# Retention and SwiGLU feed-forward in one kernel: weight chunks issued by SP, and four attention jobs and one norm moved to other places

## The chip, the cores and the metric

The kernel runs on one core of a Trainium2 chip. Its time is device microseconds of one launch, compiled kernel alone. Several executions are timed in rounds that alternate with the kernel before on the same chip; the median is quoted, with the lowest and highest run. One execution of each kernel is also recorded by the hardware profiler; moments below ("at 240.5 us") are from the start of that execution. The engines are TensorE (PE in the profile), the vector engine DVE, the scalar engine ACT, GpSimd (POOL) and SP, which here only issues transfers. A bank is the place where TensorE leaves a product until DVE or ACT has taken it out (its eviction).

## The reference

```python
# q, k, v: 8 batches x 8 heads x 576 positions x 64
scores = (q @ k.T) / sqrt(64)
Dmat = where(i >= j, gamma[h] ** (i - j), 0)       # gamma[h] = 1 - 2 ** (-5 - h)
attn = (scores * Dmat) @ v                          # retention, no softmax
x = attn.transpose(0, 2, 1, 3).reshape(4608, 512)
xn = x / sqrt(mean(x * x, -1) + 1e-6) * rms_g
g, val = xn @ w_gate, xn @ w_val                    # 512 -> 1536
out = (g * sigmoid(g) * val) @ w_out                # 1536 -> 512
```

The weights come as float64 and are turned into float32 on the chip.

## The kernel before

The attention is done in jobs (two heads of a stretch of positions), the feed-forward in units of 384 rows. Units 0 and 1 run first with plain products, while the weights still arrive; from unit 2 (the third) on the products are of the Strassen kind, seven block products in place of eight. The change touches the stretch up to the third unit's start, at about 258 us of 1147.

**Weights** come in 18 chunks of 1 MB. Each is loaded into one of four rooms, split by DVE (exponent, mantissa, sign) and ACT, and joined. A new chunk is issued once an earlier one has left its room:

```python
def load_chunks(n, queue=nc.scalar):                 # before: issued by ACT
    nonlocal n_loads
    while n_loads < min(n, len(chunks)) and waits_at.get(spare(n_loads)) is None:
        load_chunk(n_loads, queue)
        n_loads += 1

def rounding():
    for i in range(len(chunks)):
        ...                                          # exponent(i), (i + 1)
        yield from mantissa(i)                       # DVE; ends with waits_at[room] = None
        load_chunks(i + 5 if i else 0)
        ...
        join(i)
```

**Jobs.** `slot(j)` gives TensorE the values of job j-1 and the scores of job j, and DVE the weighing. `following(j)` is two things: `prepare(j+1)` (two transposes on DVE, the scaling of v on ACT) and the 13 loads of job j+2 on SP. Jobs 0 to 7 are done first. The later ones are put among the 48 steps of the up products of units 0 and 1, and among the first outs:

```python
LATER_AT = (29, 33, 37, 41, 45)

def later(step):
    if step == LATER_AT[0] - 8:
        following(2 * NHP - 1)                       # NHP = 4
    elif step in LATER_AT:
        j = 2 * NHP + LATER_AT.index(step)
        if j < LATER_JOBS:                           # LATER_JOBS = 12
            slot(j, rest=(j > 2 * NHP))
            if j + 1 < LATER_JOBS:
                following(j)
        else:
            values(j - 1)
            carried(j - 1)
```

**First outs.** `across(u)` is the last product of unit u, in seven blocks of 24 matmuls (3.9 us each). Every finished quarter is added up and transposed by DVE and stored with 8 DMAs on SP, 32 for a unit. The third unit's norm stands in `across(1)`. While GpSimd's `combine` makes the Strassen blocks of the up weights, with 12 additions for each of the two matrices:

```python
rest = across(1)
next(rest)
following(LATER_JOBS - 1)
for i, _ in enumerate(rest):
    if i == 1:
        norm_0(2)                    # ACT: four squares; DVE adds them up
        differences(0)
    elif i == 2:
        norm_1(2)                    # TensorE: mean; DVE, GpSimd: root
        diagonals(2)
    elif i == 4:
        norm_2(2)                    # DVE: four scalings, four subtractions
rest = across(0)
next(rest)
combine(1)
slot(LATER_JOBS, rest=False)
following(LATER_JOBS)
for _ in rest:
    pass
combine(0)
slot(LATER_JOBS + 1)
...                                  # third unit follows

def combine(m):
    for g in range(NG):              # NG = 3
        ...
            nc.gpsimd.tensor_tensor(out=o, in0=a, in1=b, op=op)
```

From the fourth unit on the norm's root is computed in another way (`root_1`, `root_2`): a product with ones, a guess at the root by ACT, and polishing on DVE and ACT.

Of the kernel before, what the change touches and what calls it, by code (L numbers as in the profile page):

```python
# [13 lines left out]
ALU = mybir.AluOpType  # L14
# [27 lines left out]
def kernel(  # L42
# [11 lines left out]
    nc = tc.nc  # L54
# [3 lines left out]
    NHP = H // 2  # L58
# [12 lines left out]
    K0, K1 = 2.38924456, 0.703952253  # L71
# [40 lines left out]
    rms_g = const.tile([P, NHP], F32, name="rms_g")  # L112
    rms_k = const.tile([P, NHP], F32, name="rms_k")
# [22 lines left out]
    LATER_JOBS = 3 * NHP  # L136
# [245 lines left out]
    def values(j):  # L382

        d = st[j]
        _, _, c0, c1 = jobs[j]
        av = d["av"] = [bank(f"av_{j}_{i}") for i in range(2)]
        for c in range(c0, c1):
            i, odd = divmod(c, 2)
            for e in range(2):
                mm = nc.tensor.matmul(  # L390
                    av[odd][column(j, odd, e), i * L : i * L + L],
                    lhsT=d["v"][side(odd), i, e] if c < NC - 1 else d["vt"][:, e],
                    rhs=d["ret"][side(odd), e, i],
                    start=(c < c0 + 2), stop=False, skip_group_check=True,
                )


        if j == LATER_JOBS:
            d["valued"] = nc.scalar.copy(out=tick, in_=mhalf[:1])
        else:  # L400
            d["valued"] = nc.gpsimd.memset(tick, 0.0)
        follow(d["valued"], mm)
# [39 lines left out]
    def slot(j, rest=True):  # L442

        if j > len(jobs):
            return
        if rest and j > 0:
            values(j - 1)
        if j < len(jobs):
            scores(j)
            states(j)  # L450
        if j < len(jobs):
            weigh(j)
        if j < 2 * NHP:
            sums(j)
        if rest and j > 0:
            carried(j - 1)
        if 2 * NHP <= j < len(jobs):
            sums(j)
# [10 lines left out]
    def following(j):  # L469
        prepare_next(j)  # L470
        load_next(j)
# [7 lines left out]

    def gather(u, c, sq):  # L480

        if c == NHP - 1 and u > 2:
            nc.vector.scalar_tensor_tensor(
                out=t_of[u], in0=t_of[u], scalar=EPS * DM / P, in1=sq, op0=ALU.add, op1=ALU.add
            )
        elif c:
            nc.vector.tensor_tensor(out=t_of[u], in0=t_of[u], in1=sq, op=ALU.add)
        else:
            t_of[u] = sq

    def norm_0(u):
        for c in range(NHP):
            gather(u, c, square(u, c))

    def norm_1(u):

        ms = bank(f"ms_{u}")
        for s in range(NS):
            nc.tensor.matmul(
                ms[:, s : s + 1], lhsT=t_of[u][:, s * P : s * P + P], rhs=mean_w,  # L500
                start=True, stop=True,
            )
        r = tmp.tile([P, NS], F32, tag="r", name=f"r_{u}", bufs=1)
        nc.vector.tensor_scalar(out=r, in0=ms[:, :NS], scalar1=EPS, scalar2=None, op0=ALU.add)
        nc.gpsimd.tensor_tensor(out=r, in0=r, in1=mhalf.to_broadcast([P, NS]), op=ALU.pow)
        t_of[u] = r
# [36 lines left out]
    def diagonals(u):  # L543
        r = t_of[u]
        t_of[u] = temp(f"diag_{u}")
        for s in range(NS):
            nc.vector.tensor_scalar(
                out=t_of[u][:, s * P : s * P + P], in0=ident, scalar1=r[:, s : s + 1],
                scalar2=None, op0=ALU.mult,
            )  # L550

    def norm_2(u):



        x = x_of[u]
        g = rms_k
        rb = t_of[u]
        if u < 3:
            g = rms_g  # L560
            rb = bank(f"rb_{u}")[:, :U]
            nc.tensor.matmul(rb, lhsT=ones, rhs=t_of[u], start=True, stop=True)
        for c in range(NHP):
            nc.vector.scalar_tensor_tensor(
                out=x[:, c], in0=x[:, c], scalar=g[:, c : c + 1], in1=rb,
                op0=ALU.mult, op1=ALU.mult,
            )
        if u < 2:
            return
        b11, b12 = x[:, :2, :HU], x[:, :2, HU:]  # L570
        b21, b22 = x[:, 2:, :HU], x[:, 2:, HU:]
        t = ffn.tile([P, 3, 2, HU], F32, tag="sums", name=f"sums_{u}")
        t2, t3, t4 = (t[:, i] for i in range(3))
        for o, a, b in ((t3, b22, b12), (b12, b12, b11), (t2, b22, b12), (t4, b21, t2)):
            nc.vector.tensor_tensor(out=o, in0=a, in1=b, op=ALU.subtract)

        t_of[u] = b11, b21, b12, t4, t2, t3, b22
# [97 lines left out]
    def keep(blk, t):  # L675
        nc.sync.dma_start(out=w_blocks[blk], in_=t)
# [27 lines left out]
    def differences(u):  # L704

        h = h_of[u]
        b11, b12, b22 = h[:, :NH, :HU], h[:, :NH, HU:], h[:, NH:, HU:]
        t1 = t1_of[u] = ffn.tile([P, NH, HU], F32, tag="t1", name=f"t1_{u}")
        for o, a, b in ((t1, b12, b11), (b12, b22, b12)):
            nc.vector.tensor_tensor(out=o, in0=a, in1=b, op=ALU.subtract)  # L710
# [146 lines left out]
    def load_chunks(n, queue=nc.scalar):  # L857
# [5 lines that stand above are left out]
# [69 lines left out]
    def rounding():  # L932

        nonlocal n_chunks
        for i in range(len(chunks)):
            if i not in exp_of and i in words_of:
                exponent(i)
                yield
            for ahead in (True, False):
                if i + 1 in words_of and i + 1 not in exp_of and i > (1 if ahead else 0):  # L940
                    exponent(i + 1)
                    yield
                if ahead:
                    yield from mantissa(i)
                    load_chunks(i + 5 if i else 0)
                    yield
            join(i)
            n_chunks += 1
            yield

    steps = rounding()
    LATER_AT = (29, 33, 37, 41, 45)

    def weights(n):

# [10 lines left out]
    def start():  # L966
# [33 lines left out]
        def later(step):  # L1000

            if step == LATER_AT[0] - 8:
                following(2 * NHP - 1)
            elif step in LATER_AT:
                j = 2 * NHP + LATER_AT.index(step)
                if j < LATER_JOBS:
                    slot(j, rest=(j > 2 * NHP))
                    if j + 1 < LATER_JOBS:
                        following(j)
                else:  # L1010
                    values(j - 1)
                    carried(j - 1)

        for j in range(2 * NHP):
            slot(j)
# [50 lines left out]
            pass  # L1066
        for blk, t in first_blocks.items():
            keep(blk, t)
        rest = across(1)
        next(rest)  # L1070
        following(LATER_JOBS - 1)
        for i, _ in enumerate(rest):
            if i == 1:
                norm_0(2)
                differences(0)
            elif i == 2:
                norm_1(2)
                diagonals(2)
            elif i == 4:
                norm_2(2)  # L1080
        rest = across(0)
        next(rest)
        combine(1)
        slot(LATER_JOBS, rest=False)
        following(LATER_JOBS)
        for _ in rest:
            pass
        combine(0)
        slot(LATER_JOBS + 1)
        load_next(LATER_JOBS + 1)  # L1090
# [18 lines left out]

    with tc.manual_schedule():  # L1110
        start()
        nc.vector.tensor_scalar(
            out=rms_k, in0=rms_g, scalar1=3.0 / 8.0 * K1, scalar2=None, op0=ALU.mult
        )
        for u in range(2, NU):
            for i in range(2 * NG):
                for n, _ in enumerate(up(u, i % 2, i // 2)):
                    if n == 2 and turns:
                        prepare_next(turns.pop())
                if i in (1, 3):  # L1120
                    fetch()
                    fetch()
                if i == 2 * NG - 1:
                    rest = across(u)
                    next(rest)
                behind(u, i)
            for i, _ in enumerate(rest):
                if i == 0 and turns:
                    prepare_next(turns.pop())
                if i == 2:  # L1130
                    behind(u, 6)
                    at, n = SLOTS[u % 3]
                    if 2 * NG - 1 in at:
                        load_next(NHP + u // 3 * 8 + n + len(at) - 1)
                elif i == 3 and u + 1 < NU:
                    root_2(u + 1)
                elif i == 4:
                    behind(u, 7)
# [27 lines left out]
```

## Time and profile before

| | before |
|---|---|
| median time, us | 1148.0 (1146.6 to 1148.8, 4 runs) |
| span of the profiled execution, us | 1147.0 |
| TensorE busy | 98 % |
| first outs start (`xo<-w_val`, L726) | 198.75 us |
| third unit's first product (L595) | 258.41 us |

TensorE is the bound: from 258 us on it hardly stands still. Two more are needed later. They are from the timelines of DVE and GpSimd (POOL) of the kernel before; the columns are start, duration, engine, line, operation, what is written and read, shapes, count, and in brackets the wait before it:

```profile
224.85 0.56 DVE L575 TENSOR_TENSOR sums<-x,sums 128x384 f32<-128x384 f32 x1
```

### The profile page before, as it was taken

How to read it: one execution, taken by the hardware profiler on the slowest of the kernel's cores; microseconds unless marked ns; L12 is line 12 of the kernel's file. 1: busy time of each engine (PE TensorE's matmuls, PEld its weight loads, DVE VectorE, ACT ScalarE, POOL GpSimd, SP SyncE). 2: the span in 40 equal slices, each digit the busy share in tenths (PEclk: the TensorE clock that was granted, in tenths of full speed). 3: DMA queues.
4: the chain of work that ended last, by engine and by line, in shares of the span. 5: the costliest groups of instructions: out<-in, count | busy, mean ns of one | idle time of the engine just before them, and what ended most of it. 6: DMA issues, size and time to landing. Idle time of an engine off the chain costs nothing.

```text
span 1147.0 us, 24779 instructions
## 1 busy us (share of the span) xinstructions
PE 1121.7 (98%) x10454; PEld 1045.3 (91%) x10454; DVE 733.4 (64%) x1452; ACT 257.8 (22%) x508; POOL 40.1 (4%) x68
## 2 busy tenths in 40 slices
PE   7899988999999999999999999999999999999998
PEld 6655645999999999999999999999999999999998
DVE  5888777747586586466766776466577576446353
ACT  5456531102211221121221121120221211120210
POOL 0100000190000000000000000000000000000000
PEclk9899998999999999999999999999999999999999
DMA  9844555434553555035345456305336413303304
GB/s 218 214 143 136 143 133 152 121 69 108 136 120 61 163 130 139 35 95 112 97 100 93 111 127 139 119 16 130 101 98 140 122 42 94 128 1 97 125 1 111
DMA packets 307039, 126.72 MB, mean 110 GB/s; under 512 B 284528, under 2 KB 289904, under 8 KB 306928
## 3 DMA queue, kind: packets, MB, share of 16 engines
q1 hardware_dynamic: 296784, 108.98, 38.9%
q10 hardware_dynamic: 10144, 16.16, 4.4%
q8 instruction: 82, 1.34, 0.5%
q14 instruction: 29, 0.24, 0.1%
HBM read 110.14 MB, written 14.94 MB: 109 GB/s over the span
## 4 chain that ended last, share of the span: by engine, by line
PE 93%; DVE 3%; DMA 2%; ACT 1%; issue 1%; SPq 0%; POOL 0%; DVEq 0%; POOLq 0%; ACTq 0%
PE x L595 14%; PE w L595 14%; PE z L595 14%; PE up L652 9%; PE xo L726 8%; PE wo L726 8%; PE zo L726 8%; PE y L595 7%; PE yo L726 4%; PE av L390 2%; PE av L412 2%; PE s L307 1%; PE s L329 1%; DMA w_gate<-in_moe_w_out_dram 1%; DMA w_out<-in_moe_w_out_dram 1%
## 5 line engine op out<-in xcount | busy, mean ns | idle before, releaser
L619 ACT COPY m<-x 128x384 f32<-128x384 f32 x60 | 28.8, 479 | 337.9 <-PE x L595 337.9
L726 PE MATMUL xo<-h,w_out 128*128 128x192 f32 x528 | 90.3, 328 | 0.0
L595 PE MATMUL w<-sums,w_val 128*128 128x192 f32 x480 | 88.7, 328 | 0.3
L595 PE MATMUL x<-x,w_val 128*128 128x192 f32 x480 | 88.8, 328 | 0.0
L595 PE MATMUL x<-x,w_gate 128*128 128x192 f32 x480 | 88.5, 328 | 0.0
L595 PE MATMUL w<-sums,w_gate 128*128 128x192 f32 x480 | 87.9, 326 | 0.0
L595 PE MATMUL z<-x,w_val 128*128 128x192 f32 x480 | 87.8, 326 | 0.0
L595 PE MATMUL z<-x,w_gate 128*128 128x192 f32 x480 | 87.8, 326 | 0.0
L726 PEld LDWEIGHTS xo<-h,w_out 128*128 128x128 f32 x528 | 85.9, 190 | 0.6
L726 PE MATMUL wo<-h,w_out 128*128 128x192 f32 x504 | 85.6, 326 | 0.4 <-DVE c_last L774 0.4
L602 DVE TENSOR_TENSOR u<-m,y 128x384 f32<-128x384 f32 x60 | 33.1, 552 | 78.6 <-PE y L595 78.6
L726 PEld LDWEIGHTS wo<-h,w_out 128*128 128x128 f32 x504 | 82.5, 190 | 0.7 <-DVE c_last L774 0.7
L595 PEld LDWEIGHTS w<-sums,w_val 128*128 128x128 f32 x480 | 79.2, 190 | 2.7 <-DVE c L602 2.7
L595 PEld LDWEIGHTS x<-x,w_val 128*128 128x128 f32 x480 | 79.2, 190 | 0.6
L595 PEld LDWEIGHTS x<-x,w_gate 128*128 128x128 f32 x480 | 79.3, 190 | 0.5
L595 PEld LDWEIGHTS z<-x,w_val 128*128 128x128 f32 x480 | 79.7, 190 | 0.0
L595 PEld LDWEIGHTS z<-x,w_gate 128*128 128x128 f32 x480 | 79.7, 190 | 0.0
L595 PEld LDWEIGHTS w<-sums,w_gate 128*128 128x128 f32 x480 | 79.5, 190 | 0.1
L602 DVE TENSOR_TENSOR h<-u,w 128x384 f32<-128x384 f32 x60 | 33.0, 550 | 69.4 <-PE w L595 69.4
L652 PE MATMUL up<-x,w_gate 128*128 128x384 f32 x192 | 65.8, 499 | 4.9 <-DVE x L435 3.6
L614 ACT ACTIVATE h<-h 128x384 f32<-128x384 f32 x90 | 47.0, 523 | 88.6 <-DVE h L602 88.6
L652 PE MATMUL up<-x,w_val 128*128 128x384 f32 x192 | 65.6, 501 | 1.3 <-DVE h L658 1.3
(189 smaller groups left out, 1783.1 us busy)
## 6 DMA issues: line engine op xcount, KB each, us to landing
w_out<-w_blocks SPq DMA_DIRECT2D x70, 768.0 KB, 4.9
out_dram<-o SPq DMA_DIRECT2D x364, 24.0 KB, 1.6
qraw<-in_q_dram SPq DMA_DIRECT2D x96, 72.0 KB, 2.6
kraw<-in_k_dram SPq DMA_DIRECT2D x96, 72.0 KB, 2.9
k<-in_k_dram SPq DMA_DIRECT2D x48, 128.0 KB, 2.9
v<-in_v_dram SPq DMA_DIRECT2D x48, 128.0 KB, 3.0
w_out<-in_moe_w_gate_dram ACTq DMA_DIRECT2D x5, 1024.0 KB, 5.8
w_out<-in_moe_w_out_dram ACTq DMA_DIRECT2D x3, 1024.0 KB, 6.0
```

What stands on the lines that cost most here:

```text
L307: nc.tensor.matmul(s[side(odd), e, i * L : i * L + L], lhsT=d["kT"][side(e), c * L : c * L + L], rhs=d["qT"][side(e), c * L : c * L + L], ...
L329: nc.tensor.matmul(o[side(e)], lhsT=d["k"][side(odd), i, e], rhs=d["v"][side(odd), i, e], start=True, stop=True,)
L390: mm = nc.tensor.matmul(av[odd][column(j, odd, e), i * L : i * L + L], lhsT=d["v"][side(odd), i, e] if c < NC - 1 else d["vt"][:, e], rhs= ...
L412: mm = nc.tensor.matmul(av[odd][column(j, odd, e), i * L : i * L + L], lhsT=d["sum"][c - 1][side(e)], rhs=d["qT"][side(e), c * L : c * L + L],
L595: nc.tensor.matmul(ps[:, i * HU : i * HU + HU], lhsT=w_up[m][:, 2 * blk + c, cut], rhs=t_of[u][blk][:, c], start=(start and i == c == 0), ...
L602: nc.vector.tensor_tensor(out=o, in0=a, in1=pairs_of(ps), op=ALU.add)
L614: nc.scalar.activation(out=o, in_=c, func=AF.Silu)
L619: nc.scalar.copy(out=s1, in_=pairs_of(x_))
L652: nc.tensor.matmul(ps[:, :U], lhsT=w_up[m][:, 4 * half + c, i * P : i * P + P], rhs=x_of[u][:, c], start=(c == 0), stop=(c == NHP - 1),)
L726: nc.tensor.matmul(ps[:, i * HU : i * HU + HU], lhsT=a[:, c, i * P : i * P + P], rhs=rhs[:, c], start=(start and i == c == 0), stop=False, ...
```

## The change

The intent: SP issues the chunks, so ACT need not stand still for them. Only two of the later jobs (8 and 9) stay among the up products, where the chunk chain leaves DVE no room. Two more (10 and 11) go among the first outs, where TensorE is full and DVE has time. The third unit's norm goes behind them, in the form that all later units use.

```diff
@@ values @@
-        if j == LATER_JOBS:
+        if LATER_JOBS - 2 < j <= LATER_JOBS:
             d["valued"] = nc.scalar.copy(out=tick, in_=mhalf[:1])
         else:
             d["valued"] = nc.gpsimd.memset(tick, 0.0)
@@ gather @@
-        if c == NHP - 1 and u > 2:
+        if c == NHP - 1 and u > 1:
@@ norm_2 @@
-        if u < 3:
+        if u < 2:
@@ rounding @@
-                    load_chunks(i + 5 if i else 0)
+                    load_chunks(i + 5 if i else 0, nc.sync)
@@
-    LATER_AT = (29, 33, 37, 41, 45)
+    LATER_AT = (33, 41)
@@ later @@
-                if j < LATER_JOBS:
-                    slot(j, rest=(j > 2 * NHP))
-                    if j + 1 < LATER_JOBS:
-                        following(j)
-                else:
-                    values(j - 1)
-                    carried(j - 1)
+                slot(j, rest=(j > 2 * NHP))
+                following(j)
@@ start @@
+        nc.vector.tensor_scalar(
+            out=rms_k, in0=rms_g, scalar1=3.0 / 8.0 * K1, scalar2=None, op0=ALU.mult
+        )
         rest = across(1)
         next(rest)
+        for i, _ in enumerate(rest):
+            if i == 0:
+                slot(LATER_JOBS - 2)
+                following(LATER_JOBS - 2)
+            elif i == 1:
+                differences(0)
+        slot(LATER_JOBS - 1)
         following(LATER_JOBS - 1)
-        for i, _ in enumerate(rest):
-            if i == 1:
-                norm_0(2)
-                differences(0)
-            elif i == 2:
-                norm_1(2)
-                diagonals(2)
-            elif i == 4:
-                norm_2(2)
         rest = across(0)
         next(rest)
         combine(1)
-        slot(LATER_JOBS, rest=False)
-        following(LATER_JOBS)
-        for _ in rest:
-            pass
+        for i, _ in enumerate(rest):
+            if i == 0:
+                slot(LATER_JOBS)
+                following(LATER_JOBS)
+            elif i == 1:
+                norm_0(2)
+            elif i == 2:
+                root_1(2)
+            elif i == 3:
+                root_2(2)
+            elif i == 4:
+                norm_2(2)
         combine(0)
```

(`rms_k` was set behind `start()` before; that line moved up. Line numbers are those of each kernel's own text.)

More of the change, by code (lines that the diff above doesn't have):

```diff
@@ L1111 @@
         start()
-        nc.vector.tensor_scalar(
-            out=rms_k, in0=rms_g, scalar1=3.0 / 8.0 * K1, scalar2=None, op0=ALU.mult
-        )
         for u in range(2, NU):
```

## The prediction

> **What bounds the kernel now.** I read the page's slices first, then the windows of the first 400 us, then what TensorE waited for, then the timelines of TensorE, ACT, DVE and the DMA queue between 100 and 262 us. The page:
>
> ```profile
> PE 1121.7 (98%) x10454; PEld 1045.3 (91%) x10454; DVE 733.4 (64%) x1452; ACT 257.8 (22%) x508; POOL 40.1 (4%) x68
> PE   7899988999999999999999999999999999999998
> PEclk9899998999999999999999999999999999999999
> ```
>
> From slice 8 on (230 us) TensorE is full and its clock is whole; the change touches nothing there. What can be won or lost lies before 260 us. In that stage the waits of TensorE from 135 us on, longest first, and two windows (columns: PE, PEld, DVE, ACT, POOL busy, PEclk, DMA share, GB/s):
>
> ```profile
> PE up L652 <- DVE x L435: 3.6, 1, 3.6
> PE av L390 <- ACT w_val L660: 3.5, 1, 3.5
> PE up L652 <- DVE h L658: 1.3, 1, 1.3
> 150.00:154.00 4.00, 4.00 (x8) 2.12 (x8) 3.86 (x9) 3.50 (x8) 0.00 (x0) 0.59 0.62 231
> 176.00:184.00 8.00, 6.71 (x80) 4.38 (x75) 6.74 (x15) 2.70 (x7) 0.09 (x1) 0.50 0.57 189
> ```
>
> So 3.6+3.5+1.3 = 8.4 us idle, and after both long gaps the clock is at half. The timelines show why the gaps are there (start, duration, then the wait before it):
>
> ```profile
> 165.78 0.37 ACTq L855 DMA_DIRECT2D w_gate<-in_moe_w_out_dram  x1
> 172.72 0.69 DVE L871 TENSOR_SCALAR w_gate<-w_gate 128x1024 uint32<-128x1024 uint32 x1 [6.98 <-DMA w_gate<-in_moe_w_out_dram]
> 173.45 1.15 ACT L887 ACTIVATE w_gate<-w_gate,least 128x1024 f32<-128x1024 uint32 x1 [10.58 <-DVE w_gate L871]
> 174.50 0.47 ACT L660 ACTIVATE w_val<-up 128x384 f32<-128x384 f32 x1
> 175.03 0.71 PE L390 MATMUL av<-ret,v 64*64 64x64 f32 x16 [3.52 <-ACT w_val L660]
> 179.20 12.95 PE L652 MATMUL up<-x,w_val 128*128 128x384 f32 x32 [1.28 <-DVE h L658]
> 198.75 4.06 PE L726 MATMUL xo<-w_val,w_out 128*128 128x192 f32 x24
> ```
>
> The last of 18 weight chunks is loaded only when an earlier one has left its staging room (165.78), lands 7 us later, is split by DVE and ACT, and the SiLU behind it in ACT's order frees a PSUM bank late. A chain of chunks, not TensorE, sets the pace from 137 to 179 us.
>
> **The Trainium skill.** "TensorE: Matmul & The Clock Gate", Part 1, says that an idle window of about 3.4 us halves the clock; the trace agrees (gaps of 3.6 and 3.5 us, then 0.59 and 0.50). The same page, under "Architectural detail", calls ACT and DVE strict FIFO; the trace agrees: the SiLU at 174.50 ran behind the 10.58 us wait. "DMA: Bandwidth & Descriptors", "Issuing engines are not separate DMA queues", says that another issuing engine saves only sequencer time; here an issue took 0.37 us on ACT, and what counts is rather what it waits for and stands behind. Nothing in the profile before tests that for SP.
>
> **Part 1: chunks issued by SP.** ACT loses ten issues of about 0.4 us, and no longer stands still until DVE frees the staging room. That alone frees no bank at 172 us: ACT would then wait at the exponent's activation for the same landing. On SP a chunk stands behind the 13 loads of q, k and v of a job. Such a set took 108.62 to 117.13, 151.61 to 159.19 and 204.55 to 212.60: 8 us. From the order of emission, chunk 14 comes right behind the set for job 9, which moves from step 21 to step 25. (Step n: four products into one bank, 2.66 us; step 29 ends at 129.75.) DVE's two transposes for job 8 then end at 121, the first frees the room at 120.6, the set runs to 128.5 and chunk 14 lands at about 134 (5 us after its issue; chunk 14 took 4.8 before). DVE gets to it at 130 and stalls 4 us. TensorE doesn't: five banks give it steps 30 to 34.
>
> **Part 2: jobs 8 and 9 at steps 33 and 41, none at 29, 37 and 45.** Before, job 8 at step 29 cost DVE 3.3 us (0.76+0.27+0.91+0.28 for weights and sums, 1.1 for transposes), and jobs 9 and 10 some 4.5 us each, all inside the chunk chain. Walking the chain on with durations of the trace (0.6 + 0.6 + 1.23 + 1.22 + 1.2 for a chunk's five DVE steps, 5.1 from issue to landing): chunk 15 issued 138.9, lands 144; chunk 16 issued 147.9, lands 152.9; job 8 on DVE to 151.2; chunk 16 freed at 161; SP has by then issued job 10's set (150.7 to 158.7), so chunk 17 goes at 161.1 and lands 166.2, against 165.78 and 172.7 before, when it shared the DMA engines with job 12's set. Its SiLU ends at 168.5. TensorE has run steps 30 to 41 with job 8's 1.0 us between and 0.8 us of waiting for a bank, to 163.5. So the two gaps become one of about 4.5 us. Then as before: 2.9 us for the rest of the job at half clock, a wait for the product with h (DVE, 173.1), 12.95 for steps 42 to 45, and 5.3 for the last two steps, without the 1.4 us of job 11's values: the first outs start at **191.4 instead of 198.75**, a gain of 7.3 us.
>
> **Part 3: two jobs among the first outs.** From there TensorE is full, so what is put there costs. Across(1): seven products of 3.9 = 27.3, plus job 10 at 1.7 (141.24 to 142.93 before). Then job 11 1.7, a product 3.9, job 12 with job 11's values about 1.9, two products 7.8. The sum, 27.3+1.7+1.7+3.9+1.9+7.8, is 44.3: TensorE stands before the new norm's product at 191.4+44.3 = 235.7. Before, the same stretches held 1.4 us for the norm's two small products and 1.2 for job 12's scores, 2.6 in all, against 5.3+0.65 now.
>
> **Part 4: the norm behind them.** Here I expect the gain to go. Job 13's loads stand on SP behind the 32 stores of the first outs, and the norm's squares stand on ACT behind the scaling of job 13's v. Lines of before that size this:
>
> ```profile
> 204.55 2.94 SPq L156 DMA_DIRECT2D qraw<-in_q_dram  x4
> 210.85 0.99 SPq L224 DMA_DIRECT2D v<-in_v_dram  x2
> 213.80 0.51 ACT L285 ACTIVATE v<-v,gv 128x256 f32<-128x256 f32 x1 [8.81 <-DMA v<-in_v_dram]
> 217.59 16.95 SPq L763 DMA_DIRECT2D out_dram<-o  x32
> 203.22 1.76 ACT L477 ACTIVATE sq<-x 128x384 f32<-128x384 f32 x4
> ```
>
> The first out result is there 2.4 us after the fourth product (as 217.56 against 215.18 before): 191.4+17.3+2.4 = 211.1. Thirty-two stores take 16.95: SP is free at 228. The set of job 13 issues v 6.3 us later (210.85-204.55), v lands 2.9 after that (213.80-210.85): 237.2. Scaling ends at 239.1, four squares 1.8, the last addition 0.6: **241.5**. TensorE idles 241.5-235.7 = **5.8 us**, is throttled for some 4 us after it (2 us lost), then the product 0.65, four products 15.6, job 13 2.25 (256.16 to 258.41): the third unit starts at 262.0 instead of 258.41. DVE is done with the norm by then: it has 15.6 us for some 12 us of additions, roots and scaling. So **+3.6 us**: 1147.4+3.6 = 1151.0 us. In one sum: -7.3 (part 2) +3.4 (part 3: 5.95-2.6) +7.8 (part 4) = +3.9, the same within my rounding.
>
> **Rivals.** (a) The norm is not held up, because job 13's loads get out between stores or the squares are ready in time: -7.3+3.4 = -3.9, about 1143.5. For it: ACT ran its scaling early elsewhere (177.32 for a transpose at 203.75). Against it: SP's stores ran with no gap for 16.95 us, and loads are emitted behind them. (b) SP's line makes the chunk chain later, not earlier: if a load set takes the 9 to 11 us that the one from 133.56 to 145.10 took, chunk 14 and all after it come 3 us later and chunk 17 is held too; the gain of part 2 halves: about 1155. For it: a set waits on landings. Against it: fewer transfers overlap now. (c) The chain gets shorter than I think since ACT is never blocked: the gap at 163.5 vanishes (4.5 us and 2 of clock), and with my part 4 the sum is 1144.5. Against it: DVE still waits for chunk 15 and 17 to land, whoever issues them.
>
> **Range and chances.** The terms are each sure to 2 or 3 us, and two of them cancel. Rivals (a), (b) and (c) end at 1143.5, 1155 and 1144.5, so 8 in 10 lie in 1142 to 1156. Two per cent is 23 us; the whole idle and throttled time before 260 us that is in play is some 14 us on either side, so chances: faster 0.01, same 0.98, slower 0.01.
>
> **What would show each step.** Part 1: chunk 14 issued by SP right behind 13 loads, near 128.5, and DVE waiting some 4 us for its landing. Part 2: no gap near 146; one gap of 4 to 5 us near 164 released by ACT's SiLU; first out at about 191. Part 4: a gap of about 6 us before the product with ones over sq, released by ACT or DVE, ACT waiting for v before the squares, and PEclk at 0.5 behind it; the third unit's first product at about 262. I am wrong if that gap is under 2 us, if the first outs start after 195, or if anything past 262 us differs by over 1 us.

## More of the kernel before

```profile
225.98 16.86 POOL L930 TENSOR_TENSOR w_val<-w_val 128x512 f32<-128x512 f32 x12 [13.68 <-PE wo L726]
```

The last subtraction of the third unit's norm ends at 225.4 us. The first twelve additions of `combine` begin at 225.98 us. Before the change, the norm was over when GpSimd began.

## The result, and the profile after

The changed kernel took 1156.3 us (1155.1 to 1157.8, 4 runs) against 1148.0. The ratio is 1.0074, 95 % interval 1.0057 to 1.0092: slower by 0.7 %, "the same" by the 2 % rule, and 0.3 us above the range.

| | before | predicted | after |
|---|---|---|---|
| median time, us | 1148.0 | 1151.0 | 1156.3 |
| profiled span, us | 1147.0 | | 1154.2 |
| first outs start, us | 198.75 | 191.4 | 187.64 |
| TensorE stands before the norm's product, us | | 5.8 | 7.76 |
| third unit's first product, us | 258.41 | 262.0 | 262.78 |
| ACT's copy for the third unit's fourth group, us | 289.80 | +3.6 | 296.46 (+6.66) |

The page of the changed kernel, busy times and the clock's row of its slices:

```profile
PE 1121.1 (97%) x10448; PEld 1045.9 (91%) x10448; DVE 738.6 (64%) x1453; ACT 259.4 (22%) x512; POOL 40.1 (3%) x66
...
PEclk9899999989999999999999999999999999999999
```

Beside the second slice, which is low in both, the slice with a lower clock moved from the seventh (172 to 201 us) to the ninth (231 to 260 us): one trouble went, another came. TensorE's busy time, in which slow products count in full, is equal (1121.1 against 1121.7), so the loss shows as waits. Its waits from 160 to 300 us in the changed kernel (what it waited for: total, times, longest):

```profile
PE ms L513 <- DVE sq L483: 7.8, 1, 7.8
PE av L390 <- ACT w_val L660: 4.4, 1, 4.4
PE up L652 <- DVE h L658: 1.3, 1, 1.3
PE z L595 <- DVE x L435: 1.0, 1, 1.0
PE x L595 <- DVE c L736: 0.6, 1, 0.6
```

Of the two gaps of 3.6 and 3.5 us before the first outs one is left, of 4.4. The 7.8 us ahead of the norm's product are new, and so are the last two lines, which stand at the third unit's start. TensorE's timeline of the changed kernel:

```profile
167.88 0.71 PE L390 MATMUL av<-ret,v 64*64 64x64 f32 x16 [4.45 <-ACT w_val L660]
...
172.05 15.75 PE L652 MATMUL up<-x,w_val 128*128 128x384 f32 x48 [1.28 <-DVE h L658]
187.64 4.06 PE L726 MATMUL xo<-w_val,w_out 128*128 128x192 f32 x24
...
240.50 1.62 PE L513 MATMUL ms<-sq,ones 128*128 128x384 f32 x2 [7.76 <-DVE sq L483]
241.91 6.14 PE L726 MATMUL yo<-h,w_gate 128*128 128x192 f32 x24
...
262.78 1.57 PE L595 MATMUL x<-x,w_gate 128*128 128x192 f32 x8 [0.59 <-DVE c L736]
```

And why the squares came late: SP's queue, then ACT, both of the changed kernel.

```profile
128.60 0.54 SPq L855 DMA_DIRECT2D w_gate<-in_moe_w_out_dram  x1
...
160.70 0.38 SPq L855 DMA_DIRECT2D w_gate<-in_moe_w_out_dram  x1
...
207.76 18.29 SPq L763 DMA_DIRECT2D out_dram<-o  x32
...
232.82 0.99 SPq L224 DMA_DIRECT2D v<-in_v_dram  x2
```

```profile
235.56 0.51 ACT L285 ACTIVATE v<-v,gv 128x256 f32<-128x256 f32 x1 [11.93 <-DMA v<-in_v_dram]
...
237.25 1.74 ACT L477 ACTIVATE sq<-x 128x384 f32<-128x384 f32 x4
```

The 32 stores hold SP from 207.76 to 226.05; only then can the next job's loads go. Its v is issued at 232.82 and ACT, which has waited 11.93 us for it, scales it from 235.56 on. The squares stand behind the scaling in ACT's order, though their input was written by 226.4. Then the clock, in windows of four microseconds (length, then PE, PEld, DVE, ACT, POOL busy, granted clock, DMA share, GB/s):

```profile
240.00:244.00 4.00, 3.50 (x9) 2.93 (x10) 0.99 (x3) 1.10 (x2) 0.00 (x0) 0.50 0.69 150
244.00:248.00 4.00, 4.00 (x20) 4.00 (x19) 0.47 (x1) 0.52 (x1) 0.47 (x1) 0.74 0.00 0
```

Half clock in the first window and for 2.1 of the second window's 4 us ((1 - 0.74) / 0.5 x 4): the block product `yo` takes 5.97 us from start to start (241.91 to 247.88) instead of 3.9.

Last, DVE and GpSimd at the end of the norm in the changed kernel:

```profile
251.83 1.52 DVE L538 SCALAR_TENSOR_TENSOR ms<-e,sq 128x384 f32<-128x384 f32 x1
...
258.61 1.51 DVE L575 TENSOR_TENSOR x<-x 128x384 f32<-128x384 f32 x1
...
261.70 0.56 DVE L575 TENSOR_TENSOR sums<-x,sums 128x384 f32<-128x384 f32 x1
```

```profile
234.66 3.95 POOL L930 TENSOR_TENSOR w_gate<-w_gate 128x512 f32<-128x512 f32 x3
247.53 13.72 POOL L930 TENSOR_TENSOR w_gate<-w_gate 128x512 f32<-128x512 f32 x9 [8.93 <-issue]
```

The same subtraction takes 1.51 us while GpSimd adds beside it and 0.56 once GpSimd is done (261.25). GpSimd stood from 238.6 to 247.53. The profile names no releaser; the blocks that it writes are read by `across(0)`'s first four products, and it went on 0.5 us before the last of them (`yo`) ended at 248.05, so this is probably what held it.

### The profile page after: what moved, and what is told of

Read it like the earlier page. It is cut to its first block, busy times and chain, and to the rows that moved or that the text cites. A ratio compares the mean times of both kernels' runs of the same rounds, so it can differ in the third digit from the quotient of the medians.

```text
span 1154.2 us, 24764 instructions
## 1 busy us (share of the span) xinstructions
PE 1121.1 (97%) x10448; PEld 1045.9 (91%) x10448; DVE 738.6 (64%) x1453; ACT 259.4 (22%) x512; POOL 40.1 (3%) x66
## 4 chain that ended last, share of the span: by engine, by line
PE 88%; DVE 6%; DMA 3%; ACT 1%; issue 1%; SPq 1%; POOL 0%; DVEq 0%; POOLq 0%; ACTq 0%
PE w L595 13%; PE x L595 13%; PE z L595 13%; PE xo L726 8%; PE zo L726 8%; PE wo L726 8%; PE up L652 7%; PE y L595 7%; PE yo L726 4%; PE av L390 2%; PE av L412 1%; PE s L307 1%; DMA w_gate<-in_moe_w_out_dram 1%; PE s L329 1%; DVE w_gate L908 1%
## 5 line engine op out<-in xcount | busy, mean ns | idle before, releaser
L652 PE MATMUL up<-x,w_val 128*128 128x384 f32 x192 | 62.7, 487 | 1.3 <-DVE h L658 1.3
```

The costliest lines, as they stand in the source:

```text
L652: nc.tensor.matmul(ps[:, :U], lhsT=w_up[m][:, 4 * half + c, i * P : i * P + P], rhs=x_of[u][:, c], start=(c == 0), stop=(c == NHP - 1),)
```

## The experiments

Twelve kernels ran, five rounds each, all correct, in four groups that each had their own runs of the kernel before. "After" is the changed kernel.

| kernel | median (lowest to highest), us | ratio to before, 95 % |
|---|---|---|
| after | 1156.3 (1155.1 to 1157.8) | 1.0074 (1.0057 to 1.0092) |
| squares_first | 1149.45 (1149.0 to 1150.9) | 1.0025 (1.0008 to 1.0042) |
| sp_only | 1155.18 (1154.2 to 1156.6) | 1.0072 (1.0056 to 1.0087) |
| act_issue | 1152.99 (1150.6 to 1154.7) | 1.0049 (1.0032 to 1.0065) |
| set_early | 1153.06 (1150.2 to 1153.5) | 1.0046 (1.0030 to 1.0063) |
| root_first | 1148.94 (1146.6 to 1150.1) | 1.0012 (0.9995 to 1.0029) |
| act_root_first | 1143.60 (1142.1 to 1147.0) | 0.9976 (0.9959 to 0.9992) |
| stores_split | 1161.77 (1160.3 to 1161.9) | 1.0124 (1.0104 to 1.0144) |
| act_root2_first | 1145.10 (1144.8 to 1145.6) | 0.9983 (0.9969 to 0.9998) |
| old_norm | 1145.29 (1144.0 to 1146.7) | 0.9978 (0.9963 to 0.9993) |
| after_combine_behind | 1155.57 (1153.5 to 1156.8) | 1.0070 (1.0055 to 1.0086) |
| combine_behind | 1141.05 (1139.9 to 1142.1) | 0.9943 (0.9928 to 0.9959) |
| act_root_again | 1144.91 (1143.8 to 1146.2) | 0.9979 (0.9964 to 0.9994) |

### squares_first: are the squares late because of what stands ahead of them on ACT?

```diff
             if i == 0:
                 slot(LATER_JOBS)
-                following(LATER_JOBS)
             elif i == 1:
                 norm_0(2)
+                following(LATER_JOBS)
```

> The changed kernel with job 13's preparation (scaling of v, transposes, next loads) emitted behind the third unit's squares instead of ahead of them. Theory A (the 7.76 us gap before the norm's product comes from the squares standing on ACT behind the scaling of job 13's v, whose load stands on the DMA queue behind 32 stores): the squares run at about 226.5 when job 11's x is written, are added up by 230, the gap is under 1 us, no half clock behind it, the third unit starts at about 253 instead of 262.8, and the time falls by 8 to 10 us, to about 1147. Rival B (the gap comes from DVE: job 12's sums and the additions themselves, or x of job 11 being late): the gap stays above 5 us and the time within 2 us of the changed kernel's.

Measured: 1149.45 us, ratio 1.0025 against 1.0074 for after: 6 to 7 us less. The squares ran from 224.84 to 228.3 us, and the gap fell from 7.76 to 0.31. But a wait of 2.1 us came up two products later. Waits of TensorE and one line of ACT, squares_first:

```profile
PE wo L726 <- DVE h L739: 2.1, 1, 2.1
...
PE ms L513 <- DVE sq L483: 0.3, 1, 0.3
```

```profile
237.68 0.56 ACT L515 ACTIVATE sq<-ms,guess 128x384 uint32<-128x384 uint32 x1
```

The norm's product was there at 235.3, yet ACT made the guess at the root only at 237.68, since the scaling of v now stood before that. The wait for v's loads had moved by one step of the norm. The mechanism of the gap is thereby shown: nothing else was changed and the gap went. The edit moves two transposes of DVE as well, but in after DVE stood 3.66 us for ACT's squares behind them, so ACT's wait was the one that counted. The gain is below the 8 to 10 us expected, in part because of the new wait.

### sp_only: what does SP as the issuer do by itself?

```diff
 # in the kernel before, nothing else changed
-                    load_chunks(i + 5 if i else 0)
+                    load_chunks(i + 5 if i else 0, nc.sync)
```

> The kernel before with nothing changed but the chunks of weights issued by SP. Theory A (a chunk stands behind a job's 13 loads): chunk 15 goes some 4 us later than 137.46 and chunk 17 some 6 us later than 165.78, since both are emitted right behind a set; the first outs start 5 to 9 us after 198.75 and the time rises by 5 to 10 us. Rival C (ACT standing still at the issues was the cost, so SP helps by itself): chunk 17 not later, the first outs at or before 198.75, time equal or up to 4 us shorter.

Measured: 1155.18 us against 1147.46 for the kernel before in the same rounds (ratio 1.0072), some 8 us slower: the first outs began at 204.01 us instead of 198.75. SP's queue and TensorE in sp_only:

```profile
172.57 0.54 SPq L855 DMA_DIRECT2D w_gate<-in_moe_w_out_dram  x1
```

```profile
180.97 0.71 PE L390 MATMUL av<-ret,v 64*64 64x64 f32 x16 [10.98 <-ACT w_val L660]
```

The last chunk, which ACT had issued at 165.78, goes 6.8 us later, because on SP it stands behind 13 loads of a job that wait for their own rooms. The gap ahead of job 11's values grows from 3.5 to 11 us. That is rival (b) of the prediction, in the kernel before. It shows the sign of part 1: SP as the issuer costs.

### act_issue and set_early: what does it cost in the changed kernel?

act_issue gives the chunks back to ACT; set_early leaves them on SP but puts job 8's preparation and job 9's loads at step 21 again, where they were before:

```diff
 # act_issue, in after
-                    load_chunks(i + 5 if i else 0, nc.sync)
+                    load_chunks(i + 5 if i else 0)
```

```diff
 # set_early, in after
-            if step == LATER_AT[0] - 8:
+            if step == LATER_AT[0] - 12:
```

> The changed kernel with the chunks issued by ACT again, all else kept. Theory A: chunk 14 goes at about 123 instead of 128.60 and DVE's 3.08 us wait for it vanishes, the chain is some 3 us shorter, the wait before job 9's values falls from 4.45 to 1 or 2 us and the first outs start at 183 to 185 instead of 187.64: 2 to 4 us faster than the changed kernel. Rival C (SP's issue is what brought the first outs from 198.75 to 187.64): the first outs start after 190, and it is 2 us or more slower than the changed kernel.

> The changed kernel with job 8's preparation and job 9's loads back at step 21 (four steps earlier), so that chunk 14 is not behind the set, chunk 13 is. Theory A: chunk 14 issued at about 122 to 123, DVE does not wait for it, the first outs start at 184 to 186, 1 to 4 us faster than the changed kernel. If chunk 14's place does not matter: no difference, or chunk 13 is the late one and DVE waits there instead.

Measured: 1152.99 and 1153.06 us, ratios 1.0049 and 1.0046 against 1.0074, both 3 us faster than after. Chunk 14 goes at 121.66 us, from ACT (set_early: 121.62, from SP) against 128.60 in after, and the last chunk at 155.79 (156.65) against 160.70. The gap ahead of job 9's values falls from 4.4 to 1.4 us in act_issue (1.3 in set_early), and the first outs begin at 182.85 (185.14) instead of 187.64. Two different edits that both take the 13 loads from in front of chunk 14 give the same moment of issue and the same gain. So it is the place in SP's order that costs, not SP itself. And the gap ahead of the norm's product stayed as it was, 7.77 and 7.75 us: it moved along with the first outs.

### root_first: behind the root's first step

```diff
 # in after
             if i == 0:
                 slot(LATER_JOBS)
-                following(LATER_JOBS)
 ...
             elif i == 2:
                 root_1(2)
+                following(LATER_JOBS)
```

> The changed kernel (SP issues) with job 13's preparation behind the squares and behind the root's first half too. In the run with the squares first the root's first activation ran at 237.68, 2.6 us after its product began, behind the scaling of job 13's v, and the product wo waited 2.15 us for DVE. Theory A (ACT's order behind job 13's v is the whole cost): the activation follows its product at once, the 2.15 us wait is gone and DVE reaches the unit's scaling 2 us earlier, so 2 to 4 us faster than squares_first, about 1146 to 1147.5. Rival D (DVE, slowed while GpSimd combines, is what makes it late): the wait before wo stays at 1 us or more and the time within 1 us of squares_first.

Measured: 1148.94 us, 0.5 us less than squares_first (expected 2 to 4: a miss); the intervals of the ratios, 1.0012 and 1.0025, overlap. The guess ran right behind the product, at 235.82, and the wait for `h` fell from 2.1 to 0.8 us. But the wait for the last results at the third unit's start rose from 0.6 to 1.4. DVE had become the next bound, which is what the rival in the expectation said of the time, though not of the wait before `wo`.

### act_root_first: both repairs together

It is root_first with the chunks issued by ACT (the edit of act_issue).

> The same with the chunks issued by ACT as in the kernel before: the best version that the experiments point to. If the two costs are separate, the gains add: 3 us from the issues (act_issue against the changed kernel) and 9 to 11 us from the order, so about 1143 to 1145, 2 to 4 us faster than the kernel before and 12 us faster than the changed kernel. If the time won before the first outs is swallowed again at the third unit (DVE crowded there), it comes to 1146 or more.

Measured: 1143.60 us, ratio 0.9976. The two gains add, since one is earned before the first outs and one behind them. This is a little faster than the kernel before. Run again unchanged later (act_root_again) it gave 1144.91 and 0.9979.

### stores_split: do the stores hold the loads?

```diff
 # in after
-                queue = nc.scalar if u == NU - 1 and i % 2 else nc.sync
+                queue = nc.scalar if u in (1, NU - 1) and i % 2 else nc.sync
```

> The changed kernel with every other store of the first outs (unit 1) issued by ACT, so SP is free before it may load for job 13. Theory A (job 13's loads stand behind 32 stores on SP): the loads start at about 222.5, when the transposes free their room, instead of 226.16, and the gap before the norm's product falls from 7.8 to about 4 to 5 us; 3 to 4 us faster than the changed kernel. If the loads' own time or DVE is what counts, the gap stays at 7 us or more.

Measured: 1161.77 us, over 5 us slower than after where 3 to 4 us less were expected. The gap did fall, from 7.8 to 4.8 us, as expected. But that is no success. Sixteen stores kept ACT's queue for 17.16 us (210.25 to 227.41), and DVE had to wait for a buffer that they read from. DVE's timeline, stores_split:

```profile
224.94 0.58 DVE L748 STREAM_TRANSPOSE o<-c 128x384 f32<-128x384 f32 x1 [4.88 <-DMA out_dram<-o]
```

All of DVE's work behind it came late, its transposes of job 12's q and k too: they began at 228.68 us instead of 221.55, and TensorE waited 2.5 us for the transposed k. The loads for job 13 need the room that these transposes free, so they went no earlier: at 229.53 us, against 226.16 in after. The norm's product came at 246.63 instead of 240.50; the gap before it is shorter only because TensorE came later still. So the run does not test what it was made for: that the stores hold the loads is read from SP's queue, where the loads follow the last store at once. It shows that ACT is not the place for the stores, and a limit that I had not seen: in after, the room for q is free at 222.3 us, so with no stores ahead at all the loads could go only 3.8 us sooner than 226.16.

### act_root2_first: one step further behind

In act_root_first, `following(LATER_JOBS)` stands behind `root_2(2)`, at i == 3.

> As act_root_first, with job 13's preparation one product later still, behind the root's second half. Theory A expects no more than 1 us of difference from act_root_first, since ACT's part of the norm is then already ahead of it in both; more than 1 us slower would say that job 13's transposes or scaling are now too late for its scores.

Measured: 1145.10 us against 1143.60. The intervals of the two ratios overlap (0.9983 and 0.9976). Within the scatter it makes no difference, and nothing more can be read from it.

### old_norm: is it the norm's new form?

In act_root_first, the third unit gets the earlier form of the norm again, in the new place:

```diff
-        if c == NHP - 1 and u > 1:
+        if c == NHP - 1 and u > 2:
 ...
-        if u < 2:
+        if u < 3:
 ...
-                root_1(2)
+                norm_1(2)
 ...
-                root_2(2)
+                diagonals(2)
```

> act_root_first with the third unit's norm made as in the kernel before (mean product, power on GpSimd, three diagonals, product with ones) instead of by the root's five DVE operations. In act_root_first the third unit starts 9.2 us before that of the kernel before, and 2.4 us of it are given back by 290 us, with TensorE waiting for DVE (1.4, 1.0, 0.8, 0.2 us). Theory E (the root's five operations, 5 us of DVE with GpSimd beside, crowd DVE there): waits for DVE before wo and at the third unit's first products fall by 1 us or more in sum, and the time by 1 to 3 us, to 1141 to 1142.5. Rival F (job 13's own work and the late evictions do it, or the power on GpSimd stands behind combine(1) and costs TensorE a wait before the product with ones): same time within 1 us, or slower.

Measured: 1145.29 us, ratio 0.9978: no gain. Two of DVE's waits went, but TensorE had to wait 1.2 us for the diagonals, and once more for 1.8 us with no releaser that the profile shows. The form of the norm made no measurable difference as a whole; without that last stop it might have gained a microsecond.

### after_combine_behind and combine_behind: is it GpSimd beside the norm?

These came last, when about 2 to 3 us behind the third unit's start were still without a cause. GpSimd's second `combine` is split: the four additions that the third unit's first group needs stay where they are, the other eight wait for the norm's last subtraction.

```diff
-    def combine(m):
-        for g in range(NG):
+    def combine(m, groups=range(NG), behind=None):
+        for g in groups:
 ...
-                nc.gpsimd.tensor_tensor(out=o, in0=a, in1=b, op=op)
+                done = nc.gpsimd.tensor_tensor(out=o, in0=a, in1=b, op=op)
+                if behind is not None:
+                    follow(done, behind)             # a dependency
+                    behind = None
 ...
-        combine(0)
+        combine(0, range(1))
+        combine(0, range(1, NG), normed[2])          # norm_2's last subtraction
```

combine_behind is act_root_first with this edit, after_combine_behind is after with it, and act_root_again is act_root_first as the control in the same group.

> Theory G (GpSimd beside the norm costs the rest): in the changed kernel GpSimd's second combination of weights, held up by the gap until 247.5 us, runs to 261.2 beside the last part of the third unit's norm, and the subtractions of that norm take 1.51 us instead of 0.56. Here eight of its twelve instructions are put behind the norm's last subtraction. G expects the four subtractions at 0.56 us each, the norm done some 3 us earlier, the waits of 0.6 and 1.0 us of TensorE behind 262 us gone, and 1.5 to 2.5 us less than the changed kernel's, ratio to the kernel before about 1.0055. Rival H (the waits have another cause, DVE being behind anyway because its result evictions wait for the slow product): the subtractions get shorter but the time stays within 0.5 us of the changed kernel, ratio 1.007 to 1.008.

> The same edit on the best version so far (loads behind the first root, chunks by ACT). There the second combination runs from 230.2 to 248.3 us over the whole of the norm on DVE. Theory G: the root's two long instructions fall from 1.44 and 1.52 to about 0.55, the subtractions from 1.51 to 0.56, DVE is done with the norm some 4 to 5 us earlier, TensorE's waits of 1.4 us (for the last results' eviction) and 1.0 us (for the values) at the third unit's start go or halve: 1.5 to 2.4 us faster than the same version without the edit in this call, about 1141.5. Rival H: no faster by more than 0.5 us.

> The best version so far once more, unchanged, as the control of the run before on the same chip: ratio to the kernel before 0.996 to 0.999, waits of 1.4 and 1.0 us at the third unit's start.

Measured: combine_behind 1141.05 us against 1144.91 for the control, ratios 0.9943 and 0.9979 with intervals apart: 3.9 us, more than expected. In the control GpSimd works beside the whole norm, though no gap holds it up there:

```profile
232.42 18.06 POOL L930 TENSOR_TENSOR w_gate<-w_gate 128x512 f32<-128x512 f32 x12
```

TensorE's waits in the control:

```profile
PE x L595 <- DVE c L736: 1.4, 1, 1.4
...
PE z L595 <- DVE x L435: 1.0, 1, 1.0
```

and in combine_behind, whose lines are numbered two further on from there, the same wait for z, with that for x gone:

```profile
PE z L597 <- DVE x L435: 0.6, 1, 0.6
```

DVE and GpSimd in combine_behind:

```profile
239.47 0.57 DVE L538 SCALAR_TENSOR_TENSOR ms<-e,sq 128x384 f32<-128x384 f32 x1
...
244.49 0.56 DVE L577 TENSOR_TENSOR x<-x 128x384 f32<-128x384 f32 x1
```

```profile
246.31 10.60 POOL L932 TENSOR_TENSOR w_gate<-w_gate 128x512 f32<-128x512 f32 x8 [7.65 <-DVE sums L577]
```

What took 1.52 and 1.51 us (in the control as in after) takes 0.57 and 0.56, and the waits of 1.4 us (x) and 0.8 us (`h`, in the control) are gone. From the first outs to the third unit's third product (`z`) the trace is 3.0 us shorter (67.59 against 70.56). Another 1.2 us comes later, because a stop of TensorE with no releaser (0.95 us in the control) is absent, so not all of the 3.9 us need be GpSimd's. It is the fastest version, 0.6 % faster than the kernel before.

after_combine_behind gave 1155.57 us: 0.7 us less than after by the medians, 0.0004 by the ratios, where 1.5 to 2.5 us were expected. By its time this one is a miss. Its trace shows what the edit does: all four subtractions at 0.56 us, and the waits for x and z gone (0.6 and 1.0 in after). From ACT's copy in the second out product (222.79 us in after, 226.05 here, before the edit acts) to the third unit's fourth group (296.46 and 297.35) it is 2.4 us shorter. But it had come to the first outs 3.25 us later than the profiled execution of after, with the same code up to there. About 1.2 us of that was there at 74 us. The rest is nearly all half clock: behind a gap of the same length (4.60 and 4.45 us) the 48 up products took 17.67 us here and 15.75 in after. In squares_first, root_first and stores_split, whose code is that of after up to there too, they took 17.99, 17.54 and 17.75. So this early stage alone scatters by over 3 us between executions, as much as the edit is worth. Why its 2.4 us do not show in the medians stays open; the granted clock was 0.985 to 0.987 in all six runs, that of after 0.987 to 0.991.

## Why the prediction was wrong

Its class was right, its sign was right, and its mechanism in part 4 was right; the time was 5.3 us above it (0.6 of that because it started from 1147.4 and not 1148.0). In one sum, from the two profiled executions:

| step | predicted | measured | how measured |
|---|---|---|---|
| part 2, first outs earlier | -7.3 | -11.1 | 187.64 - 198.75 |
| part 3, two jobs among the first outs | +3.4 | +4.4 | 75.14 us from first outs to third unit, less before's 59.66, less part 4 |
| part 4, the norm's gap, its clock, and the wait at the third unit's start | +7.8 | +11.1 | 7.76 + 2.07 + 0.69 + 0.59 |
| third unit's start | +3.6 | +4.4 | 262.78 - 258.41 |
| behind the third unit's start | 0 | +2.8 | 1154.2 - 1147.0 - 4.4 |

**The step that failed** is the last: "DVE is done with the norm by then: it has 15.6 us for some 12 us of additions, roots and scaling." DVE was done with the norm at 262.26 us, but TensorE had arrived at 262.19 and stood 0.59 us for the eviction that comes next in DVE's order; more waits followed. The prediction had named anything over 1 us behind 262 us as a sign of being wrong, and the difference is 2.8. Two things were left out. First, DVE could not use the whole of that time, since its next work in order was the eviction of `yo`, and it stood 3.61 us for that product, at half clock. Second, GpSimd's additions now ran beside the norm, which had moved into their time. The gap is not what brought them together: in squares_first, without the gap, they run from 219.0 to 254.6 us, beside the whole norm.

After_combine_behind gives the size: L535, L538, L739 and three of the subtractions took 0.33, 0.95, 0.60, 0.20, 0.95 and 0.95 us less there, 4.0 us in all. Combine_behind shows that this costs time: 3.9 us there by the medians, of which the trace places 3.0 at the third unit's first products. In the changed kernel itself the edit took away the waits of 0.59, 0.97 and 0.16 us in the trace, but the medians show 0.7 us, so what it costs there in time stays open. In the kernel before the two never met. Of the 2.8 us, three waits of TensorE just behind the third unit's start are 1.5: 0.97 and 0.16 for DVE, and 0.37 with no releaser. Counted by how much later each next product starts, they come to 2.3; the remaining 0.5 lies behind 296 us and was not traced.

That the third unit started within 0.8 us of the 262.0 predicted is luck: part 2 was 3.8 us better than predicted, and parts 3 and 4 were 1.0 and 3.3 worse.

**Part 1** was placed to within 0.7 us: chunk 14 at 128.60 (predicted 128.5), the last at 160.70 (161.1). DVE waited 3.08 us for chunk 14 (predicted some 4). But the part was priced as nearly free, and the runs price it at 3 us (act_issue, set_early). The prediction had the 13 loads ahead of chunk 14 and the 4 us that DVE stands for them in its own walk, and didn't ask what the walk gives without them.

**Part 2** was right in kind: one gap, 4.45 us long (predicted 4.5), released by ACT's SiLU. The gain was larger for two reasons. The products behind the wait for `h` began at 172.05, not at the 173.1 assumed. And the 12.95 us for four steps were copied from the kernel before, where the half clock lasted to 184 us; here it ended by 172, and all six steps took 15.6 us, against 18.25 assumed. That second part is not to be relied on: in the four other executions with the same code up to there (squares_first, root_first, stores_split, after_combine_behind) the first outs began at 188.9 to 190.9 us, so the gain was 8 to 10. (The medians differ by 8.3 us and the profiled executions by 7.2 because of which runs were profiled: before's took 1148.79, the longest of its four, after's 1155.91, a little under its median.)

**Part 3** was close: jobs 10, 11 and 12 cost 1.68, 1.68 and 1.98 us among the first outs (sized 1.7, 1.7 and 1.9). The rest is some 0.1 to 0.2 us for each product next to a job. No run puts these jobs back alone; the figures are read from the traces.

**Part 4** had the mechanism, and squares_first shows it. The moment was predicted within 1.0 us, 241.5 against 240.50, but by two errors that cancel. From the first outs on, the norm's product came after 52.9 us (predicted 50.1), and TensorE was free for it after 45.1 (predicted 44.3), so the gap was 2 us longer. Of the 2.8 us, 1.5 is SP, which was held 18.4 us by the stores and not 16.95, and 0.9 is the end of the additions behind the squares (1.5 us, not 0.6). The larger gain of part 2 did not lengthen the gap, since the stores themselves wait for the first outs: in act_issue the first outs began 4.8 us earlier than in after, and the norm's product came 52.85 us behind them again. The clock was priced at 2 us and cost 2.07 in `yo` and 0.69 in the norm's own product.

**The rivals.** (a), no hold-up, and (c), no gap at 163, did not come. (b) came close in time (1155) for another reason: the load sets took 7 us, not 9 to 11, and chunk 17 was not held.

**The range** came from the rivals' end points. None of them let DVE be late with the norm, so everything behind the third unit's start was taken as zero with no error.

## What to carry to other kernels

When work moves to a stretch where the bounding engine is full, list what each of the other queues does in that stretch, GpSimd too, and re-price every instruction that will now run beside it; durations from the old place do not come along. When a queue is issued in order, a cheap instruction costs what stands ahead of it: putting a job's loads behind the norm's work and the chunks on the other queue turned a loss of 0.7 % into a small gain, with the same jobs in the same places. And for a gap, ask what each of its ends hangs on: here both hung on the first outs, so time won before them was kept and the gap stayed as long (7.76 us in after, 7.77 in act_issue, which was 4.8 us ahead).

## What the Trainium skill lacked or had wrong

- "SBUF — State Buffer", section "Who interferes with whom", says that a DVE instruction with two inputs in SBUF contends with a GpSimd instruction that reads SBUF. The trace agrees, and the page gives no duration for this pairing: DVE subtractions on 128x384 float32 took mostly 1.51 us beside GpSimd additions on 128x512 (the first of the four 0.76) and 0.56 without them. GpSimd's own additions took 1.27 us at the median and 2.4 at most. Putting eight GpSimd instructions behind the norm made combine_behind 3.9 us faster than its control.
- "DMA: Bandwidth & Descriptors", section "Issuing engines are not separate DMA queues", calls the time to initiate a DMA usually small relative to the DMA. Not so here: 32 stores of 24 KB held SP for 18.29 us (0.57 each), and the median one landed 1.6 us after its issue. The section also doesn't say that a load waits behind whatever stands ahead on its issuing engine, which put the last chunk's issue 6.8 us later in sp_only.
- "TensorE: Matmul & The Clock Gate", Part 1, says that the window is free-running and the moment of transition therefore varies by half a microsecond. Here more varied than that. Every gap of 3.18 us (sp_only) or more was followed by half clock; one of 2.15 in squares_first was not. Gaps of 1.2 to 1.4 us with one of 2.08 some 2 us later were followed by half clock in three executions (set_early, old_norm, combine_behind) and not in four (act_issue, act_root_first, act_root_again, act_root2_first). Behind gaps of 4.2 to 4.7 us the same 48 products took 15.75, 17.54, 17.67, 17.75 and 17.99 us in five executions. Half clock lasted from 174 to 184 us in the kernel before, with a second wait of 1.28 us inside.
- No page looked at sizes the stops of TensorE that have no releaser in the profile: 0.37 us in the changed kernel, 1.84 in old_norm. A transfer of instructions lies beside the latter in the record of the DMA queues; that it is the cause is a guess.
